# Turning x of eight pairs with transposing transfers instead of TensorE

## The chip, the cores and the metric

The kernel runs on one core of a Trainium2 chip. The metric is device time in microseconds, as the median of several runs; smaller is better. Besides these runs there is one execution taken by the profiler, from which every duration below comes.

## What is computed

Two steps, one behind the other. Attention within chunks of 64 tokens, and then a token mixer without a softmax:

```python
# q, k, v: (8 batches, 8 heads, 576 tokens, 64)
scores = scale * np.matmul(q_c, k_c.transpose(0, 1, 2, 4, 3))   # per chunk of 64
attn = softmax(scores)                                          # 1e-9 is added to the sum
out = np.matmul(attn, v_c)                                      # back to (8, 8, 576, 64)
# x: heads side by side, (8, 576, 512)
wq, wk = x @ w_q, x @ w_k                                       # 512 -> 64
W_tok = scale * np.einsum('bsd,btd->bst', wq, wk)
mixed = np.einsum('bst,btd->bsd', W_tok, x)
y = np.maximum(mixed, 0.0) @ w_out                              # (8, 576, 512) float32
```

## The kernel before

**Pairs.** The work is cut into twenty pairs `u` (a batch and a block of 256 tokens, two "blocks" of 128 each). Two batches give five pairs: two whole pairs of the first, one rest pair that holds the last 64 tokens of both, two whole pairs of the second. So 2, 7, 12 and 17 are the rest pairs, and 8 and 9, 10 and 11, 13 and 14, 15 and 16 are the whole pairs of batches 3, 4, 5 and 6.

**Steps of a pair.** `turns` brings q and k into SBUF with the head dimension on the partitions (turned on TensorE, L379, copied out of PSUM as `qbd` and `kt`). `attention` makes the scores on TensorE (L400), the row maximum and the subtraction on VectorE (L413, L424, L420 for rest pairs), the exponential on ScalarE (L434), turns the exponentials on TensorE (L446), copies them out as `et`, multiplies by v in two steps for a whole pair (L477), and after each step computes denominator, reciprocal and product on VectorE (L490, L494, L504). The products are `xs[u]`, f16, 128 tokens x 2 blocks x 512 features.

**The projection.** `project` needs x with features on the partitions. For each pair its inner function `turn` makes a TensorE step `xT` (L528, eight 128x128 transposes into PSUM) and a copy `xt` out of PSUM by ScalarE or VectorE. The pairs of one batch share one `xt` tile. Step `pj` (L545) multiplies it by `wqk` in four matmuls; `wt`, `wkT` and `wkn` follow.

**Mixing.** `mixing` makes the gram matrix of a batch on TensorE (L599) and copies it as `g16`; `mix_out` makes the mix in two halves (L639) and the relu `rm`; `outs` makes the outputs (L688, four matmuls a group), copies them into one of eleven `osb` buffers, and `send` issues the stores: two for each whole pair (L711) and two for each rest pair (L705), nearly all from SyncE.

**Order.** Nothing is scheduled at run time. Every step gets a number in the order in which it is created, and the string `ORDER` lists all steps: `p` on TensorE, `a` on ScalarE, `v` on VectorE, `s` a send on SyncE, `t` a send on ScalarE's queue, `i` a filler matmul. The number behind `p` is the PSUM bank. Each engine runs its steps strictly in the order of this list and waits for what a step needs. The last lines of the function read it:

```python
    for e in ORDER.split():
        what, eng, *at = re.split(r"([ipavst])", e, maxsplit=1)
        ...
        n.emit(*{"p": (), "a": ("ACT",), "v": ("DVE",)}[eng])
```

**Loads.** The string `LOADS` orders the loads of q, k and v (`Q8`, `K8`, `v8`: of pair 8), which GpSimd issues and which cast from f32 to f16 on the way. A load is issued as soon as its buffer has been read by the pair that held it, in that order and no other.

Of the kernel before, what the change touches and what calls it, by code (L numbers as in the profile page):

```python
# [11 lines left out]
F32 = mybir.dt.float32  # L12
# [58 lines left out]
1v 0a i7.256 i6.256 i5.256 i7.256 i6.256 i5.256 i7.256 i6.256 i5.256 i7.256 i6.256 i5.256 i7.256 i6.256 i5.256  # L71
i7.256 i6.256 i5.512 i7.256 i6.256 7p0 8v 3a 2v 6a 9a i7.512 i6.512 i5.512 i7.512 i6.512 i5.512 i7.256 10p1 11a
i7.512 i6.512 i5.512 i7.256 12p0 26p7 13v 29p6 88p5 14v 28a 27a 30a i4.512 i3.512 i2.512 i4.512 91p7 15a i6.256
31p0 92v 32v 89a i6.512 i3.512 i7.512 53p4 16p7 33v 17a 56a i3.512 i2.512 18p6 90a 54v 22p2 19v 23v 34a 24v 55v
20v 25v i1.512 i0.512 57p4 93p0 58v 35p5 21v 107p2 36a 59v 45p3 109a 94v 110p5 108a 60a i4.512 41p6 95v i2.256
61p4 111a 62a 46a i2.512 63p4 96a 37p0 64v 42v 65v 38v 43v i2.512 153p3 39v 44v 97p2 155a 40v 112p6 66v 47p0
98a 154a 113v 67p2 156p1 68a 48a i5.512 69p2 114v 157a 49p0 158p4 70v 50v 115a 159v 103p2 71p0 99p6 72a 51p0
116p1 52a 4a 172p0 117a 104v 160v 100v 175p1 73p4.5 173v 105v 174a 101v 106v 176a 102v 74v 75a 118p6 122p0 5a
78p4 161a 123v 119v 124v 125v 120v 76p2 77a 121v 126p0 199p1 79v 177p6 200a 128p2 127a 178v 162p3 202a 129a
163a 201a 130p2 179v 131a 180a 203p3 84p1 204v 82p2 205v 85a 168p6 206a 132p3 181p1 169v 83v 164p4 170v 182a  # L80
234p2 165v 133v 166v 171v 134p3.1 236a 167v 235a 183p6 136a 187p4 135a 191p2 188v 184v 189v 207p3 190v 185v
139p0 137p4 140a 192v 186v 138v 237p2 253p6 208a 238a 209p0 255a 193p7 210v 239p4 211v 194a 212v 256p2 254a
240v 213p7 195p6 214a 257v 149p0 241v 215p7 145p2 216a 196a 217p7 150v 242a 258p4 218v 302p6 259v 299p7 303a
318p3 300a 146v 86p6 301a 260v 320a 197p2 304p0 198a 243p7 319a 305v 87a 87s 244a 143p2 345p3 306v 219p6.4 348a
144a 321p7 347v 221a 220a 249p0 245p4 261a 346v 246v 250v 80p6 251v 247v 248v 322a 349p3 81a 81s 323p4 222p6
350v 223a 252v 262p2 351v 224p0 263a 324v 147p3 225a 272p6 325v 380p2 273a 383p7 352a 382v 268p4 264p0 265v
151p6 381a 266v 269v 270v 267v 384a 230p2 326a 271v 385p0 274p7 353p4 231v 307a 386v 327p2 275a 308p5 328a
276p7 354v 309a 387v 148a 148s 314p4 277a 226p2 315v 316v 152a 152s 317v 278p7 310p0 279a 333p4 227a 311v 399p6
334v 312v 335v 313v 280p7.3 402p2 336v 281v 329p0 403a 355p4 330v 228p7 337p2 401a 331v 356v 332v 357v 282a
338a 400a 358v 339p3 283p0 285p4 340v 284v 359p2 286a 341p6 232p3 360v 388a 342v 295p4 404p0 296a 343p6 361p2  # L90
405v 141p4 344a 362a 363p2 448p6 142a 142s 364v 406v 365p2.5 229a 229s 464p4 449a 233v 233s 445p7 367a 366a
407a 389p5 447v 368p2 446v 370p0 390a 369v 289p6 371a 408p5 466v 395p2 409a 391p0 376p7 392v 465a 396v 393v
397v 394v 450p4 398v 377a 290a 467p0 451v 410p2 468a 414p6 374p1 411v 412v 452v 297p0 375a 418p1 453a 413v
469p4 415v 416v 293p2 419a 417v 470v 454p1 491p3 420p6 471v 298a 298s 455a 291p7 421a 294a 493v 460p4 456p0
472a 492v 422p2 457v 458v 494v 459v 495p3 423a 287p6 461v 462v 496v 424p2 473p0 425a 497v 378p1 474a 463v 498a
475p2 288v 288s 479p4 379a 379s 526p0 480v 292a 292s 481v 426p1.6 482v 529p7 476v 427a 428v 527a 477v 429p4
478v 530a 483p6 430v 528a 431p2 499p7 432a 531p0 484v 545p4 532v 548p5 500a 546a 501p6 485p2 549a 502v 533v
439p3 547a 486a 550p4 503v 504v 534a 372p2 551v 441p6 535p0 505p1 373a 373s 442a 552v 487p2 506a 536a 507p1
488a 508v 537p4 541p6 553a 538v 542v 509p2 489p1 437p0 490v 539v 543v 440a 540v 554p1 510a 544v 511p2.3 555a
438a 438s 556p6 560p4 512v 513a 561v 564p1 557v 558v 562v 516p2 565a 435p0 559v 563v 517a 514p6 566p1 515v  # L100
433p2 567a 568p1 443p3 569a 434a 570p1 524p6 444a 444s 571v 436a 436s 572p1.7 522p0 574v 573a 525v 577p2 575p6
523a 523s 578a 520p0 576v 518p1 521v 581p6 583p0 519a 519s 584a 584s 579p1 580v 582a 582s 589p2 587p0 585p6
590a 591p1 586a 592v 588a 588s 592s 586t
"""


# [1 line left out]
def kernel(  # L108
# [10 lines left out]
    nc = tc.nc  # L119
# [3 lines left out]
    C, P, R, G = 64, 128, 2, 32  # L123
    NF = DM // P
# [23 lines left out]
    wqk = const.tile([P, NF, 2, DH], F16, name="wqk")  # L148
# [3 lines left out]
    wo = const.tile([P, NF, DM], F16, name="wo")  # L152
# [22 lines left out]
    def home(tag, shape, dtype=F16):  # L175
        return work.tile(shape, dtype, name=tag, tag=tag, bufs=HOMES[tag])
# [116 lines left out]
    def either(n):  # L293
        return {"ACT": act(n), "DVE": vec(n)}
# [4 lines left out]
    def copy(eng, to, of):  # L299
        (nc.vector.tensor_copy if eng == "DVE" else nc.scalar.copy)(to, of)  # L300

    st, xs = {}, {}
# [210 lines left out]
    def project(us):  # L513

        b, m = pairs[us[0]]
        ni = 1 if m is None else 2
        wide = len(us) * ni * P
        bp, bw = Banks(1), Banks(1)
        made = []

        def turn(n, u):
            bt = Banks(1)

            def pe_t():
                tx = in_banks(bt, ni * NF * C, F16)[:, 0].rearrange("p (f i s) -> p f i s", f=NF, i=ni)
                for i in range(ni):
                    for f in range(NF):
                        nc.tensor.transpose(tx[:, f, i, :], xs[u][:, i, 2 * f : 2 * f + 2, :], ident[:])  # L528
# [188 lines left out]
    for u, (b, m) in enumerate(pairs):  # L717
        made = turns(u)
# [23 lines left out]
_INS = ['q', 'k', 'v', 'moe_w_q', 'moe_w_k', 'moe_w_out']  # L742
_OUTS = [((8, 576, 512), 'float32')]
# [25 lines left out]
```

## Time and profile before

| | |
|---|---|
| median of 3 runs | 137.56 us (137.22 to 137.69) |
| the profiled execution's own time | 137.94 us |
| its span, first to last instruction | 136.1 us |
| mean granted TensorE clock | 0.994 |
| TensorE busy | 121.7 us, 89% |
| VectorE busy | 109.3 us, 80% |
| ScalarE busy | 100.5 us, 74% |
| GpSimd busy (issuing loads) | 74.5 us, 55% |
| transfers | 25.08 MB, mean 184 GB/s |
| SyncE's queue (hardware_dynamic) | 7328 packets, 10.36 MB |
| GpSimd's queue (software_dynamic) | 78752 packets, 14.29 MB |

Busy time is the union of an engine's instructions; matmuls overlap one another, so their mean duration is longer than the step from one to the next. The chain of waits gives the step: each piece of it is the time for which that line held the end back. In the profile, PE is TensorE, PEld its weight load, DVE VectorE, ACT ScalarE, POOL GpSimd, and SPq SyncE's queue. A row of a group ends with the idle time of its engine just before it, and with what ended that idleness.

### The profile page before, as it was taken

How to read it: one execution, taken by the hardware profiler on the slowest of the kernel's cores; microseconds unless marked ns; L12 is line 12 of the kernel's file. 1: busy time of each engine (PE TensorE's matmuls, PEld its weight loads, DVE VectorE, ACT ScalarE, POOL GpSimd, SP SyncE). 2: the span in 40 equal slices, each digit the busy share in tenths (PEclk: the TensorE clock that was granted, in tenths of full speed). 3: DMA queues.
4: the chain of work that ended last, by engine and by line, in shares of the span. 5: the costliest groups of instructions: out<-in, count | busy, mean ns of one | idle time of the engine just before them, and what ended most of it. 6: DMA issues, size and time to landing. Idle time of an engine off the chain costs nothing.

```text
span 136.1 us, 4949 instructions
## 1 busy us (share of the span) xinstructions
PE 121.7 (89%) x2120; PEld 82.6 (61%) x2120; DVE 109.3 (80%) x210; ACT 100.5 (74%) x175; POOL 74.5 (55%) x96
## 2 busy tenths in 40 slices
PE   6998879986899999999999999996999999999910
PEld 4565656865646677676668667663568766544500
DVE  5635999999898899999999979999699998636220
ACT  6358469867998777998995789865878999576600
POOL 7966989978987859995539348935600000000000
PEclk9999999999999999999999999999999999999997
DMA  3999999999999999999999999999999833619883
GB/s 85 284 180 163 172 165 172 165 168 180 174 173 171 181 175 165 175 161 245 256 176 178 281 165 152 177 242 255 202 176 225 282 76 98 154 37 250 269 256 113
DMA packets 86245, 25.08 MB, mean 184 GB/s; under 512 B 78928, under 2 KB 81744, under 8 KB 86224
## 3 DMA queue, kind: packets, MB, share of 16 engines
q0 software_dynamic: 78752, 14.29, 129.5%
q1 hardware_dynamic: 7328, 10.36, 25.7%
q8 instruction: 16, 0.26, 0.7%
q10 hardware_dynamic: 144, 0.13, 0.3%
q14 instruction: 5, 0.04, 0.1%
HBM read 29.62 MB, written 9.44 MB: 287 GB/s over the span
## 4 chain that ended last, share of the span: by engine, by line
PE 60%; DVE 13%; ACT 10%; DMA 6%; issue 5%; POOL 2%; POOLq 0%; DVEq 0%; ACTq 0%
PE ps L688 22%; PE ps L379 7%; DMA qk<-in_q_dram 6%; PE ps L528 5%; PE ps L477 5%; PE ps L400 4%; PE ps L545 4%; PE ps L639 4%; DVE xs L504 4%; PE ps L446 3%; ACT es L434 2%; DVE mx L413 2%; PE ps L599 2%; PE ps L732 2%; ACT et L300 1%
## 5 line engine op out<-in xcount | busy, mean ns | idle before, releaser
L688 PE MATMUL ps<-wo,rm 128*128 128x512 f16 (+1 forms) x148 | 35.8, 374 | 0.1
L230 POOL DMA_DIRECT2D v_all<-in_v_dram x33 | 28.7, 882 | 10.4 <-PE ps L528 4.2
L413 DVE TENSOR_REDUCE mx<-ps 128x16 f32<-128x1024 f32 (+1 forms) x20 | 22.2, 1108 | 3.0 <-PE ps L400 3.0
L504 DVE TENSOR_TENSOR xs<-ps,rec 128x512 f16<-128x512 f32 x36 | 23.9, 684 | 0.4
L434 ACT ACTIVATE es<-sh 128x1024 f16<-128x1024 f32 (+1 forms) x20 | 19.3, 972 | 1.8 <-DVE sh L424 1.7
L688 PEld LDWEIGHTS <-rm 128*128 128x128 f16 x148 | 13.1, 98 | 12.2 <-issue 0.4
L379 PE MATMUL ps<-ident,qk 128*64 128x128 f16 x512 | 19.4, 221 | 1.2 <-DMA qk<-in_q_dram 0.6
L424 DVE TENSOR_TENSOR sh<-ps,mx 128x1024 f32<-128x1024 f32 x16 | 19.6, 1224 | 0.5
L300 ACT COPY osb<-ps 128x512 f32<-128x512 f32 (+1 forms) x28 | 15.3, 574 | 4.6 <-PE ps L688 4.0
L379 PEld LDWEIGHTS <-qk 128*64 128x64 f16 x512 | 15.8, 110 | 4.5 <-DMA qk<-in_q_dram 1.3
L300 ACT COPY qbd<-ps 64x512 f32<-64x512 f32 (+1 forms) x28 | 15.7, 565 | 2.9 <-PE ps L379 1.7
L216 POOL DMA_DIRECT2D qk<-in_q_dram x15 | 13.6, 908 | 4.1 <-PE ps L379 1.6
L216 POOL DMA_DIRECT2D qk<-in_k_dram x15 | 13.5, 902 | 3.6 <-DMA qk<-in_k_dram 2.7
L661 ACT ACTIVATE rm<-ps 128x1024 f16<-128x1024 f32 (+1 forms) x12 | 13.7, 1138 | 2.0 <-PE ps L639 1.8
L300 ACT COPY et<-ps 128x512 f32<-128x512 f32 (+1 forms) x19 | 10.4, 550 | 5.5 <-PE ps L446 5.3
L732 PE MATMUL ps<-ones 128*128 128x512 f16 (+1 forms) x48 | 11.9, 383 | 1.2 <-DVE ones L155 1.2
L400 PEld LDWEIGHTS <-qbd 128*128 128x128 f16 x288 | 10.4, 98 | 3.5 <-DVE qbd L300 0.9
L446 PE MATMUL ps<-ident,es 128*128 128x128 f16 x144 | 11.2, 219 | 1.3 <-issue 1.3
L400 PE MATMUL ps<-kt,qbd 128*128 128x64 f16 x288 | 11.5, 193 | 0.7 <-DVE qbd L300 0.5
L528 PE MATMUL ps<-ident,xs 128*128 128x128 f16 x144 | 11.2, 220 | 0.9 <-DVE xs L504 0.9
L477 PE MATMUL ps<-v_all,et 64*64 64x65 f16 x576 | 10.4, 195 | 1.8 <-DVE xs L504 1.1
L477 PEld LDWEIGHTS <-et 64*64 64x64 f16 x576 | 7.8, 107 | 6.6 <-issue 2.6
(56 smaller groups left out, 177.1 us busy)
## 6 DMA issues: line engine op xcount, KB each, us to landing
out_dram<-osb SPq DMA_DIRECT2D x31, 256.0 KB, 4.5
v_all<-in_v_dram POOLq DMA_DIRECT2D x31, 128.0 KB, 6.7
qk<-in_q_dram POOLq DMA_DIRECT2D x15, 256.0 KB, 7.9
qk<-in_k_dram POOLq DMA_DIRECT2D x15, 256.0 KB, 8.0
out_dram<-osb SPq DMA_DIRECT2D x9, 128.0 KB, 4.1
v_all<-in_v_dram POOLq DMA_DIRECT2D x10, 64.0 KB, 7.8
osb<-in_q_dram SPq DMA_DIRECT2D x1, 512.0 KB, 4.1
osb<-in_k_dram SPq DMA_DIRECT2D x1, 512.0 KB, 5.1
```

Of the source, the lines that this page charges most:

```text
L216: nc.gpsimd.dma_start(qk[u][:, t], rows)
L230: nc.gpsimd.dma_start(v_all[on, slot[u] + i, :, 0:D], v[b, :, of, :].rearrange("h p d -> p h d"))
L300: (nc.vector.tensor_copy if eng == "DVE" else nc.scalar.copy)(to, of)
L379: nc.tensor.transpose(tp[half(o), j, :, r, :], of, ident[:])
L400: nc.tensor.matmul(sp[:, i, j, c ^ turned(u, i), :], lhsT=st["qb", u][:, j, x].rearrange("p o s -> p (o s)"), rhs=st["kt", u][:, j, x * C ...
L413: nc.vector.tensor_reduce(mx[:], scores(), axis=AX.X, op=ALU.max)
L424: nc.vector.tensor_tensor(out=sh[:].rearrange("p x (g r) -> p x r g", r=R), in0=in_banks(bs, 512).rearrange("p i (x r g) -> p (i x) r g", ...
L434: nc.scalar.activation(es[:].rearrange("p x s -> p (x s)"), st["sh", u][:].rearrange("p x s -> p (x s)"), AF.Exp, scale=scale_attn,)
L477: nc.tensor.matmul(to[half(k ^ i), i if ni == 2 else w, x, :], lhsT=et[half(k), i, h // 2, h % 2, :], rhs=v_all[half(k), slot[u] + i, h, 0:W],
L504: nc.vector.tensor_tensor(out=to, in0=xp()[:, :, :, 0:D], in1=by, op=ALU.mult)
L528: nc.tensor.transpose(tx[:, f, i, :], xs[u][:, i, 2 * f : 2 * f + 2, :], ident[:])
L688: nc.tensor.matmul(in_banks(bo, wide)[:, 0], lhsT=st["rm", key][:, f, at_tok + i * P : at_tok + i * P + P], rhs=wo[:, f, s], start=(f == 0 ...
```

## The change

For the pairs 8, 9, 10, 11, 13, 14, 15 and 16 the step `xT` on TensorE and the copy `xt` are replaced by one step `xd`: two transposing transfers issued by SyncE, one for each block of 128 tokens, which read `xs[u]` and write the same `xt` tile, SBUF to SBUF. Each moves 128 x 512 f16 values, 128 KB. The other twelve pairs are turned as before. In `ORDER` such a step has the letter `d`. There are eight steps fewer, so the numbers behind the first carried pair differ from those before. The lists `LOADS` and `ORDER` are new in full; the engines that copy out of PSUM are chosen anew with them, and there are 45 fillers where there were 48.

```diff
+CARRIED = (8, 9, 10, 11, 13, 14, 15, 16)
...
-LOADS = "Q1 K1 Q3 K3 Q2 K2 v0 Q4 K4 v1 v2 Q5 K5 wqk v3 Q6 K6 v4 Q7 K7 wo v5 Q8 v6 K8 Q9 v7 K9 Q10 K10 Q11 Q12 K11 K12 v8 Q13 K13 v9 v10 v11 Q14 K14 v12 Q15 K15 Q16 v13 K16 v14 Q17 K17 v15 Q18 v16 K18 v17 Q19 K19 v18 v19 "
+LOADS = "Q1 K1 Q3 K3 Q2 K2 Q4 K4 v0 v1 Q5 K5 v2 v3 Q6 K6 wqk v4 Q7 K7 v7 Q8 K8 v5 v6 Q9 K9 Q10 K10 wo Q12 Q11 K12 K11 v8 Q13 K13 Q17 v9 v10 v11 Q14 v12 K14 Q15 K15 K17 Q16 K16 v13 v17 v14 v15 Q18 v16 K18 Q19 K19 v18 v19 "
...
+        def room(n, u):
+
+            if ("xt", us[0]) not in st:
+                st["xt", us[0]] = home(f"xt{ni}", [P, NF, wide])
+            return st["xt", us[0]][:, :, n * ni * P : n * ni * P + ni * P]
+
         def turn(n, u):
+            if u in CARRIED:
+
+                def carry():
+                    for i in range(ni):
+                        to = room(n, u)[:, :, i * P : i * P + P]
+                        nc.sync.dma_start(to, xs[u][:, i].rearrange("p h d -> p (h d)"), transpose=True)
+
+                made.append(add("xd", {"SP": 1.0}, carry, st["x_n", u]))
+                return
             bt = Banks(1)
...
-                copy(eng, to, in_banks(bt, ni * NF * C)[:, 0].rearrange("p (f s) -> p f s", f=NF))
+                copy(eng, room(n, u).bitcast(F32), in_banks(bt, ni * NF * C)[:, 0].rearrange("p (f s) -> p f s", f=NF))
...
-        what, eng, *at = re.split(r"([ipavst])", e, maxsplit=1)
+        what, eng, *at = re.split(r"([ipavstd])", e, maxsplit=1)
...
-        n.emit(*{"p": (), "a": ("ACT",), "v": ("DVE",)}[eng])
+        n.emit(*{"p": (), "d": (), "a": ("ACT",), "v": ("DVE",)}[eng])
```

Of the new `ORDER`, the stretches around the four places where the projection takes carried pairs. Pairs 8 and 9 (`268p0` is the last v step of pair 9, `152v` and `152s` the copy and the send of rest pair 2, `274p1` the projection), then 10 and 11 (`337p4`):

```text
321p4 264p2 219p0.7 221a 379p1 80p7 220a 380a 268p0 322v 347v 323v 348a 81a 81s 324a 224p4 269v 270v 265v 271v 266v 267v
349p7 151p6 325p0 222p2 152v 152s 225a 350a 326a 223a 312p4 351p6 352v 313v 353v 314v 315v 354v 147p1 86p0 272d
273d 308p4 331p6 327p2 148v 148s 332v 333v 309v 328v 329v 334v 310v 330v 311v 87a 87s 274p1 230p0 381p6 382v
275a 398p1 395p4 276p5 355p2 439p3 399a 277a 383v 396a 397v 278p5.1 279v 280v 356a 357p2 400p6 440a 384a 231a
441a 226p5 283p0 336d 335d 337p4 385p3 401v 402v 284a 293p6 358a 338a 227v 294v 281p0 141p5 359p4 339p2 282a
```

Pairs 13 and 14 (`285p5` the last outputs of pair 8, `286a` and `286s` their copy and send, `416p5` the projection), then 15 and 16 (`473p6` the last v step of pair 16, `479p3` the projection):

```text
487p6 374p7 373a 449a 285p5 286a 286s 414d 415d 464v 488v 465v 518p4 454p2 450p0 416p5 489v 466a 467p6 455v
451v 456v 452v 453v 417v 490a 491p0 295p1 457v 492v 519a 468a 520a 418p6 469p2 493p4 419a 296a 296s 375a 375s
420p6.0 521p1 421a 422a 473p6 470v 494v 471v 495v 472v 496v 474v 475v 425p2 476v 522a 426a 523p0 524v 289p4
537p5 540p2 423p6 368p3 539a 538a 541a 497p5 478d 477d 525v 424v 542p0 431p2 543v 526a 369a 369s 290a 290s 432a
498a 479p3 480a 527p4 499p5 427p2 500a 501p5 481p3 435p6 544v 545a 528v 502v 482v 436a 529p0 533p4 546p3
```

More of the change, by code (lines that the diff above doesn't have):

```diff
@@ L72 @@
[L72 to L101, printed above, removed]
@@ new lines @@
+95v 34a i6.512 i1.256 57p7 5v 111a i6.512 18p0 22p2 23v 19v 35p4 24v 20v 58v 59v 96a 108a 36a 97p6 21v 41p4
+i7.512 37p0 42v 25v 38v 45p7 112p2 60a 39v 43v 40v 44v 113v 153p4 156p5 i1.256 61p0 155a 154a 62v 63p0 47p4
+114v 64v 98a 46a 99p6 103p2 48v 157a 115a 175p4 172p5 174a 100v 104v 105v 65v 106v 101v 102v 66v 158p6 159v
+160v 116p0 117a 176a 173a 126p1 67p2 49p3 122p4 123v 68a 50a 118p6 51p0 119v 124v 125v 120v 121v 4v 69p3 70a
+199p2 177p4 128p3 71p6 178v 161a 127a 234p1 162p7 201a 179v 202v 200v 236v 72a 52a 129a 163a 130p3 131v 73p0.4
@@ new lines @@
+168p6 180a 132p5 181p3 237p2 182a 133a 74a 238a 169v 75v 235v 170v 171v 203p1 204v 183p4 134p0.3 187p6 135a
+136a 205v 188v 189v 190v 184v 76p0 164p2 165v 185v 166v 137p6 77a 206a 138a 167v 186v 239p0 207p2 78p4 191p3
+256p6 208a 257a 297p2 299a 298a 192a 300p7 240v 241v 79v 253p6 149p0 139p4 209p2 254v 255v 210v 301a 150a 193p7
+302p0 242a 140a 211v 212v 82p6 213p2 303v 316p3 258p4 194a 83a 318a 214v 304v 259v 317v 84p7 341p6 243p2 85a
+215p7 216v 305a 6a 244a 260v 145p0 217p7 342v 218v 146a 195p3 249p4 245p0 196a 250v 246v 251v 343v 247v 248v
@@ new lines @@
+306p7 143p3 197p2 319p0 376p1 261a 252v 307v 344v 144a 262p3 345p6 346v 320a 198a 378a 263a 377a 321p4 264p2
+219p0.7 221a 379p1 80p7 220a 380a 268p0 322v 347v 323v 348a 81a 81s 324a 224p4 269v 270v 265v 271v 266v 267v
+349p7 151p6 325p0 222p2 152v 152s 225a 350a 326a 223a 312p4 351p6 352v 313v 353v 314v 315v 354v 147p1 86p0 272d
+273d 308p4 331p6 327p2 148v 148s 332v 333v 309v 328v 329v 334v 310v 330v 311v 87a 87s 274p1 230p0 381p6 382v
+275a 398p1 395p4 276p5 355p2 439p3 399a 277a 383v 396a 397v 278p5.1 279v 280v 356a 357p2 400p6 440a 384a 231a
@@ new lines @@
+441a 226p5 283p0 336d 335d 337p4 385p3 401v 402v 284a 293p6 358a 338a 227v 294v 281p0 141p5 359p4 339p2 282a
+386a 340v 442p6 458p7 460v 360a 443a 361p4.3 444p0 445v 403a 363a 142a 142s 362a 228p6 459a 229a 229s 232p3
+404p2 364p4 446v 387p0 233v 233s 388v 389v 390v 405v 365a 366p6 461p3 462v 367a 447a 287p4 391p0 406p6 410p2
+288v 411v 412v 392v 393v 394v 291p5 370p4 483p0 413v 407v 408v 484v 485v 409v 371a 292a 463p2 486a 372p4 448p5
+487p6 374p7 373a 449a 285p5 286a 286s 414d 415d 464v 488v 465v 518p4 454p2 450p0 416p5 489v 466a 467p6 455v
@@ new lines @@
+451v 456v 452v 453v 417v 490a 491p0 295p1 457v 492v 519a 468a 520a 418p6 469p2 493p4 419a 296a 296s 375a 375s
+420p6.0 521p1 421a 422a 473p6 470v 494v 471v 495v 472v 496v 474v 475v 425p2 476v 522a 426a 523p0 524v 289p4
+537p5 540p2 423p6 368p3 539a 538a 541a 497p5 478d 477d 525v 424v 542p0 431p2 543v 526a 369a 369s 290a 290s 432a
+498a 479p3 480a 527p4 499p5 427p2 500a 501p5 481p3 435p6 544v 545a 528v 502v 482v 436a 529p0 533p4 546p3
+503p6.7 534v 530v 535v 531v 536v 532v 428a 547a 505a 504v 552p2 548p4 553v 549v 554v 550v 555v 551v 429p7 508p0
@@ L104 @@
+556p6 506p2 558p4 433p5 557v 559a 509a 560p4 437p6 561a 430a 507v 562p4 516p0 434v 434s 430s 563a 564p7.1 438a
+438s 517a 565v 566v 514p0 515v 515s 567p6 569p4 512p1 568a 570v 513a 510p0 511a 511s 581p4 582v 577p1 579p6
+575p0 571p7 583p4 573p5 576v 572v 580a 580s 576s 578v 578s 584a 574v 574s 584t
 """
```

10 lines of the change are left out of this document (4 added, 6 removed).

## The prediction

> **What bounds the kernel now.** I read the page first, then busy time by stretch, the chain of work that ended last, the groups by form, and last SyncE's own queue with its transfers. In the groups by form, "128x512 f16 x36 | 23.9, 684" means 36 instructions, 23.9 us busy together, 684 ns each.
>
> ```profile
> span 136.1 us, 4949 instructions
> PE 121.7 (89%) x2120; PEld 82.6 (61%) x2120; DVE 109.3 (80%) x210; ACT 100.5 (74%) x175; POOL 74.5 (55%) x96
> PE 60%; DVE 13%; ACT 10%; DMA 6%; issue 5%; POOL 2%; POOLq 0%; DVEq 0%; ACTq 0%
> ```
>
> The same by stretch (columns: PE, PEld, DVE, ACT, POOL busy with counts, clock, DMA share, GB/s):
>
> ```profile
> 0.00:40.00 40.00, 34.20 (x626) 24.07 (x627) 32.10 (x60) 28.47 (x49) 34.17 (x47) 1.00 1.84 173
> 40.00:130.00 90.00, 87.49 (x1496) 58.55 (x1494) 76.70 (x152) 72.03 (x127) 40.32 (x49) 1.00 1.50 190
> ```
>
> From 40 to 130 us TensorE is busy 87.49 of 90 us: it runs one step after the other in the order of the list and waits 2.5 us in all. So whatever leaves TensorE's list there is worth its time, and whatever makes TensorE wait there costs its time. All eight carried pairs lie in that stretch. These are the prices of TensorE's steps, as the chain of waits lists them (start, time on the chain, what):
>
> ```profile
> 55.65 0.47 PE ps L400 x16
> 56.12 0.45 PE ps L446 x8
> 56.56 0.86 PE ps L688 x4
> 62.55 0.43 PE ps L639 x2
> 63.86 0.45 PE ps L528 x8
> 70.55 0.25 PE ps L477 x16
> 73.03 0.55 PE ps L599 x10
> 73.58 0.45 PE ps L379 x16
> 77.33 0.22 PE ps L528 x4
> 77.56 0.86 PE ps L545 x4
> 97.28 0.97 PE ps L545 x4
> 104.53 0.22 PE ps L446 x4
> ```
>
> In names: scores 0.47, turning the exponentials 0.45 (0.22 for a rest pair), a group of outputs 0.86, half a mix 0.43, turning x 0.45 (0.22), half of attention times v 0.25, the gram matrix 0.55, turning q or k 0.45, the projection 0.86.
>
> **What is removed.** Eight pairs lose their eight transposes: 8 x 0.45 = 3.6 us off TensorE, on the path. They also lose one eviction each, six of them on ScalarE:
>
> ```profile
> L300 ACT COPY xt<-ps 128x512 f32<-128x512 f32 x13 | 7.6, 585 | 1.6 <-PE ps L528 1.5
> PE ps L545 <- ACT xt L300: 0.3, 1, 0.3
> ```
>
> 6 x 0.585 = 3.5 us of ScalarE, beside TensorE's other work: in the whole run the projection waited for this eviction once, 0.3 us. I count these at nothing. If ScalarE or VectorE waits are smoothed too, the most that can come back is the 2.5 us of idleness above.
>
> **What is added.** Sixteen transfers of 128 KB on SyncE's queue, two a pair, four ahead of each of four projections. The projection is the next step on TensorE that needs them, and everything behind it in the list waits with it. No transposing transfer is in this trace. Its nearest rows are the stores of the same queue: first their issue, then issue to landing while loads still run (57 to 95 us) and while they end (95 to 122 us), then the extremes.
>
> ```profile
> 70.91 1.25 SPq L711 DMA_DIRECT2D out_dram<-osb  x2
> 72.25 1.27 SPq L705 DMA_DIRECT2D out_dram<-osb  x2
> 127.60 0.37 SPq L707 DMA_DIRECT2D out_dram<-osb  x1
> ```
>
> ```profile
> out_dram<-osb SPq DMA_DIRECT2D x12, 256.0 KB, 6.9
> out_dram<-osb SPq DMA_DIRECT2D x4, 128.0 KB, 6.2
> ```
>
> ```profile
> out_dram<-osb SPq DMA_DIRECT2D x11, 256.0 KB, 4.0
> out_dram<-osb SPq DMA_DIRECT2D x2, 128.0 KB, 2.3
> ```
>
> ```profile
> DMA to landing us min/median/max: 2.2/4.4/9.0
> ```
>
> So one issue takes 0.63 us (0.37 at the least), three ahead of the last one 1.9 us, and the landing L of a 128 KB store is 6.2 us beside the loads and 2.3 us without them. A transposing transfer stays inside SBUF, which may make it quicker than a store (I go down to 1 us), or it moves in smaller pieces, which may make it slower (up to the 9.0 us of the slowest store). I take the row of the same size and hour. What must pass before the four can be issued is read from the order, with these prices:
>
> ```profile
> L504 DVE TENSOR_TENSOR xs<-ps,rec 128x512 f16<-128x512 f32 x36 | 23.9, 684 | 0.4
> L424 DVE TENSOR_TENSOR sh<-ps,mx 128x1024 f32<-128x1024 f32 x16 | 19.6, 1224 | 0.5
> L413 DVE TENSOR_REDUCE mx<-ps 128x16 f32<-128x1024 f32 x16 | 19.5, 1217 | 3.0 <-PE ps L400 3.0
> L300 ACT COPY osb<-ps 128x512 f32<-128x512 f32 x26 | 14.7, 589 | 4.3 <-PE ps L688 3.7 <-PE ps L561 0.6
> L494 DVE RECIPROCAL rec<-den 128x8 f32<-128x8 f32 x36 | 6.3, 192 | 0.7 <-DVE den L490 0.2
> L300 DVE COPY osb<-ps 128x512 f32<-128x512 f32 x9 | 6.2, 684 | 3.8 <-ACT osb L300 2.5 <-PE ps L688 1.2
> L490 DVE TENSOR_SCALAR den<-ps 128x8 f32<-128x8 f32 x36 | 5.2, 159 | 2.7 <-PE ps L477 2.0 <-ACT g L323 0.3
> L420 DVE TENSOR_TENSOR sh<-ps,mx 128x512 f32<-128x512 f32 x4 | 2.7, 686 | 0.1
> ```
>
> **Pairs 8 and 9 (272d, 273d, projection 274p1).** Time counts from the end of 268p0, the last v step of pair 9. TensorE then has mix 0.43, turning 0.22, output 0.86, turning 0.45, mix 0.43, two v steps 0.5, two outputs 1.72, three v steps 0.75: 5.4 us, then the projection. VectorE first ends a max and two subtractions (1.22 + 0.69 + 1.22 = 3.1), the first of which could start when the scores step 321p4 ended; TensorE's steps from there to the end of 268p0 are 0.25 + 0.55 + 0.45 + 0.86 + 0.25 = 2.4, so it is 0.8 us late. Then two denominators, two reciprocals and two products (2.1) and the output copy 152v (0.68), since SyncE's list has 152s, the send of that copy, ahead of 272d: 3.5. The send is two issues, 1.27: 4.8. Three issues 1.9: 6.7. Then L. TensorE waits 6.7 + L - 5.4 = L + 1.3. The loads are at their thickest here, L = 6.2: **7.5 us**.
>
> **Pairs 10 and 11 (336d, 335d, projection 337p4).** By the same clock VectorE's products for them end at 3.5 + 2.1 + 0.7 + 3.1 = 9.4, and SyncE, after 273d (7.3) and the two sends 148s and 87s, is free at 9.8; its last of four issues starts at 11.7 and lands at 11.7 + L. TensorE, after waiting, starts 274p1 at 6.7 + L and has then at least 0.86 + 0.86 + 0.47 + 0.9 + 0.22 + 0.45 + 0.55 + 0.47 + 0.86 + 0.43 = 6.1 us before 337p4: 12.8 + L. Whatever L is, these land 1.1 us in time: **0**, hidden by the wait before. If that cover went, L - 5.2 would show, which is 1.0 us.
>
> **Pairs 13 and 14 (414d, 415d, projection 416p5).** SyncE has 286s ahead, whose last copy 286a can begin only when output step 285p5 ends. From there: copy 0.59, two issues 1.27, three issues 1.9, L: 3.8 + L. TensorE has turning 0.45 and two v steps 0.5, 0.95. It waits L + 2.8. In the run before, this projection began at 97.28 us, where the loads are ending; I take L = 5, between 6.2 and 4.0: **7.8 us**.
>
> **Pairs 15 and 16 (478d, 477d, projection 479p3).** From the end of v step 473p6 TensorE has 0.43 + 0.47 + 0.86 + 0.9 + 0.43 + 0.86 + 0.22 + 0.47 + 0.86 = 5.5 us. VectorE needs between one denominator, reciprocal and product (1.0) and three of each (3.1); I take 1.9, then 1.9 of issue, then L, and all loads are down: L = 3, a little over 2.3. The wait is L - 1.7: **1.3 us**, between 0 and 4.
>
> **The rest.** Behind the transfers on SyncE's queue stand sends (148s, 87s; 296s, 375s; 369s, 290s); nobody on TensorE waits for a send but through the eleven output buffers, and the last sends come long after. They cost nothing. The 2 MB share the engines with the loads; TensorE's waits above give the loads more time than they lose. The loads' order and the first steps are rearranged, with 45 fillers for 48. TensorE is idle 5.8 us in the first 40; the new head I count at 0, between -2 and +3. Counted over both lists, VectorE gets some copies that ScalarE had: about 5 us more on an engine busy 76.7 of 90 us, covered by the waits.
>
> **Sum.** The profiled execution took 137.94 us around its span of 136.1, 0.4 above the median 137.56. 137.94 - 3.6 + 7.5 + 0 + 7.8 + 1.3 = 150.9, so 150.5 for the runs that are timed. The likeliest case with its own range is 147 to 153.
>
> **Two rules weighed.** The trace prices eight turns at 0.45 us on TensorE and has none by transfer. The Trainium skill, "VectorE: DVE Perf Modes", section "The three transpose paths", gives 1309 ns for one 128x128 block by DMA against 390 ns on TensorE, and the rules under it advise TensorE where PSUM will do as the destination. A transfer here holds four blocks; estimated from that page, L lies between 1.3 (overlapped) and 5.2 (one by one), and the sum would be 141.0 or 152.3.
>
> The second is TensorE's clock, which falls in the trace:
>
> ```profile
> 129.00:130.00 1.00, 0.78 (x4) 0.17 (x2) 0.18 (x1) 0.60 (x2) 0.00 (x0) 1.00 0.83 270
> 134.00:134.50 0.50, 0.00 (x0) 0.00 (x0) 0.00 (x0) 0.00 (x0) 0.00 (x0) 1.00 0.67 172
> 134.50:135.00 0.50, 0.00 (x0) 0.00 (x0) 0.00 (x0) 0.00 (x0) 0.00 (x0) 0.59 0.01 4
> ```
>
> The last matmul ends at 129.8, and between 134.5 and 135 the granted clock drops to half: some 4.8 us of idleness do it. The waits of 7.5 and 7.8 us are longer. The Trainium skill, "TensorE: Matmul & The Clock Gate", section "What's actually happening", has the clock halved after an idle window of about 3.4 us and back after as long a busy one; estimated by that, two such waits lose 1.7 us each, 154.3 in the sum. The drop agrees in size; the return no row here shows.
>
> **Rivals.** *Quick transfers hidden (faster).* The three waits total 2L + 4.1 for small L; with all 2.5 us of idleness recovered the sum is even at L = 1.0, and at L = 0.5 with issues of 0.37 us (three of them 1.1 instead of 1.9, so 0.8 less at each of two places) 137.94 - 3.6 - 2.5 + 1.0 + 2.5 = 135.3. For: nothing goes to HBM. Against: no store landed under 2.2 us. Chance 0.05. *Short landing:* L = 2.3 everywhere: waits 3.6 + 5.1 + 0.6, 143.6; for it the rows after 95 us, against it those before. Chance 0.23, as 141 to 147. *Half clock:* each long wait is followed by matmuls at half speed; if that lasts as long as the fall took, 2.4 us each are lost, 155.7. Chance 0.15. *Slower than a store:* L = 9 twice, then 4: 10.3 + 11.8 + 2.3 of waits, 158.7. Chance 0.14. *The waits cancel against 3.6 us:* 0.02. The forecast keeps 0.41. Both high rivals reach from 153 to 160. 142 to 160 leaves out some 0.15.
>
> A difference under 0.3% can't be told from none here. Slower by more: 0.41 + 0.23 + 0.15 + 0.14 = 0.93; the same 0.02; faster 0.05.
>
> **What would show it.** TensorE should lose 64 of the 144 turns of L528, and the waits list should name L545 waiting for transfers into xt, two waits of 6 to 9 us, one of 1 to 2, one of none; SyncE should issue each first transfer right after the send ahead of it. Wrong would be: transfers that land under 2 us, a projection that starts without waiting, SyncE's issues over 1 us each, or VectorE as the releaser of TensorE's waits.

## The result and the profile after

The changed kernel takes 168.14 us (166.09 to 168.36, 4 runs) against 137.39: the ratio is 1.2207, with a 95% interval of 1.2142 to 1.2273. The forecast was slower, 150.5, within 142 to 160: the direction held, and the time lies beyond the range. The profiled execution is the quickest of the four, 166.09 us, with a mean granted clock of 0.94; the other three had 0.91. Where executions of one kernel fall into a quicker and a slower group, its ratio below is that of the quicker group.

First the page after: span, busy time, granted clock in forty slices, and the chain that ended last.

```profile
span 164.3 us, 4844 instructions
PE 122.6 (75%) x2053; PEld 80.1 (49%) x2053; DVE 113.9 (69%) x221; ACT 92.6 (56%) x156; POOL 74.5 (45%) x96
PEclk9999999999999999998559999999758999999996
PE 34%; DMA 19%; DVE 15%; SPq 12%; POOL 7%; issue 4%; ACT 4%; POOLq 0%; DVEq 0%
```

TensorE's share of the chain fell from 60% to 34%; transfers and SyncE's queue have 31%. The clock goes to half in two places. The waits of TensorE name the cause, and its timeline the places (start, length, what, and in brackets the idle time before it and its releaser):

```profile
PE ps L558 <- DMA xt<-xs: 23.1, 4, 10.6
PE ps L380 <- DMA qk<-in_k_dram: 2.7, 3, 2.0
```

```profile
83.83 1.87 PE L558 MATMUL ps<-xt,wqk 128*128 128x512 f16 x4 [10.55 <-DMA xt<-xs]
94.56 1.04 PE L558 MATMUL ps<-xt,wqk 128*128 128x512 f16 x4 [1.75 <-DMA xt<-xs]
121.05 1.86 PE L558 MATMUL ps<-xt,wqk 128*128 128x512 f16 x4 [7.81 <-DMA xt<-xs]
136.48 1.02 PE L558 MATMUL ps<-xt,wqk 128*128 128x512 f16 x4 [3.02 <-DMA xt<-xs]
```

All four projections with carried pairs waited: 10.55, 1.75, 7.81 and 3.02 us. The forecast had 7.5, 0, 7.8 and 1.3. SyncE's timeline shows what stood in front:

```profile
70.20 1.13 SPq L718 DMA_DIRECT2D out_dram<-osb  x2
71.37 6.10 SPq L534 DMA_TRANSPOSE xt<-xs  x4
77.59 2.67 SPq L724 DMA_DIRECT2D out_dram<-osb  x4
80.38 7.00 SPq L534 DMA_TRANSPOSE xt<-xs  x4
101.41 12.55 SPq L724 DMA_DIRECT2D out_dram<-osb  x8
114.07 5.74 SPq L534 DMA_TRANSPOSE xt<-xs  x4
130.04 5.20 SPq L534 DMA_TRANSPOSE xt<-xs  x4
```

Two stores take 1.13 us to issue, four transposing transfers 5.2 to 7.0. From issue to landing, the first eight (71 to 88 us) and the next four (114 to 120 us):

```profile
L534 SPq DMA_TRANSPOSE xt<-xs x8: 1226/1364/2446, 71.4 to 84.9; - x8
DMA to landing us min/median/max: 7.7/8.3/9.6
```

```profile
L534 SPq DMA_TRANSPOSE xt<-xs x4: 1211/1264/1811, 114.1 to 118.5; - x4
DMA to landing us min/median/max: 2.3/2.4/3.6
```

So a transposing transfer takes at least 1.21 us to issue, twice a store, and lands in 2.4 us or in 8.3, by when it goes. Landing counts from the start of the issue: the last transfer of the third group starts at 118.5, and TensorE's wait for it ends at 121.05.

### The profile page after: what moved, and what is told of

It is laid out like the page before. It is cut to its first block, busy times and chain, and to the rows that moved or that the text cites. A ratio compares the mean times of both kernels' runs of the same rounds, so it can differ in the third digit from the quotient of the medians.

```text
span 164.3 us, 4844 instructions
## 1 busy us (share of the span) xinstructions
PE 122.6 (75%) x2053; PEld 80.1 (49%) x2053; DVE 113.9 (69%) x221; ACT 92.6 (56%) x156; POOL 74.5 (45%) x96
## 4 chain that ended last, share of the span: by engine, by line
PE 34%; DMA 19%; DVE 15%; SPq 12%; POOL 7%; issue 4%; ACT 4%; POOLq 0%; DVEq 0%
PE ps L701 15%; DMA qk<-in_k_dram 10%; SPq L534 10%; DMA xt<-xs 9%; PE ps L652 4%; DVE mx L414 3%; POOL qk L217 3%; PE ps L558 3%; DVE xs L505 3%; PE ps L380 3%; PE ps L447 3%; POOL v_all L231 3%; DVE sh L425 2%; SPq L724 2%; PE ps L478 2%
## 5 line engine op out<-in xcount | busy, mean ns | idle before, releaser
L414 DVE TENSOR_REDUCE mx<-ps 128x16 f32<-128x1024 f32 (+1 forms) x20 | 22.0, 1110 | 15.2 <-PE ps L401 15.2
L558 PE MATMUL ps<-xt,wqk 128*128 128x512 f16 (+1 forms) x48 | 11.5, 366 | 23.1 <-DMA xt<-xs 23.1
L380 PE MATMUL ps<-ident,qk 128*64 128x128 f16 x512 | 18.7, 221 | 4.4 <-DMA qk<-in_k_dram 2.7
L301 ACT COPY qbd<-ps 64x512 f32<-64x512 f32 (+1 forms) x24 | 13.5, 561 | 11.5 <-PE ps L380 10.9
L380 PEld LDWEIGHTS <-qk 128*64 128x64 f16 x512 | 15.4, 110 | 8.6 <-DMA qk<-in_k_dram 3.7
L301 ACT COPY osb<-ps 128x512 f32<-128x512 f32 (+1 forms) x26 | 14.6, 578 | 7.6 <-PE ps L701 7.5
L674 ACT ACTIVATE rm<-ps 128x1024 f16<-128x1024 f32 (+1 forms) x14 | 16.8, 1207 | 3.1 <-PE ps L652 3.0
L558 PEld LDWEIGHTS <-wqk 128*128 128x128 f16 x48 | 3.9, 102 | 27.3 <-issue 23.3
L301 ACT COPY et<-ps 128x512 f32<-128x512 f32 (+1 forms) x15 | 8.2, 553 | 11.7 <-PE ps L447 11.6
L301 ACT CAST wt<-ps 128x512 f16<-128x512 f32 (+1 forms) x9 | 4.3, 481 | 17.7 <-PE ps L558 17.6
L478 PE MATMUL ps<-v_all,et 64*64 64x65 f16 x576 | 11.3, 196 | 2.3 <-ACT et L301 0.7
L478 PEld LDWEIGHTS <-et 64*64 64x64 f16 x576 | 8.6, 106 | 8.7 <-issue 4.9
```

The costliest lines, as they stand in the source:

```text
L380: nc.tensor.transpose(tp[half(o), j, :, r, :], of, ident[:])
L414: nc.vector.tensor_reduce(mx[:], scores(), axis=AX.X, op=ALU.max)
L478: nc.tensor.matmul(to[half(k ^ i), i if ni == 2 else w, x, :], lhsT=et[half(k), i, h // 2, h % 2, :], rhs=v_all[half(k), slot[u] + i, h, 0:W],
L558: nc.tensor.matmul(in_banks(bp, wide)[:, 0], lhsT=wqk[:, f].rearrange("p i j -> p (i j)"), rhs=st["xt", us[0]][:, f, :], start=(f == 0), s ...
L674: nc.scalar.activation(to, of, AF.Relu, scale=scale_moe)
```

## The experiments

In every kernel that reads ones, the projections of the eight pairs get a tile of ones for the turned x, so it leaves out what would be computed from x there. Diffs are cut; `...` stands for what is left out, and for long stretches of a list.

**1. The lists alone (e_list).** What do the new lists cost when no transfer is issued?

```diff
-                    for i in range(ni):
+                    for i in range(0):
...
-                    rhs=st["xt", us[0]][:, f, :],
+                    rhs=ones[:] if us[0] in CARRIED else st["xt", us[0]][:, f, :],
```

> The changed kernel's two lists with neither transposes nor transfers for the eight pairs: their projections read a tile of ones instead of the turned x, so the values computed there are left out. Theory (the four waits for the transfers are the loss): without them TensorE has 3.6 us of turns and 1.2 us of fillers less and some 3 us more idleness in the first 60 us than before, so 137.4 - 4.8 + 3.2 = 135.8, between 134 and 139. Rival (the new lists are slow in themselves, for instance by the order of the loads): above 145. Rival (the lists are good and only the first part lost): 133 or less.

Measured: 140.2 us, ratio 1.0229 (1.0172 to 1.0285). Neither end: the 27.9 us between this and the changed kernel are the transfers', but the lists without turns are 2.7 us slower than the kernel before, which does all turns. TensorE's busy time by stretch, here and before (first column after the length):

```profile
0.00:60.00 60.00, 50.31 (x987) 35.86 (x988) 52.84 (x99) 39.76 (x68) 49.62 (x66) 1.00 1.86 170
```

```profile
0.00:60.00 60.00, 53.73 (x1030) 38.29 (x1031) 50.88 (x96) 44.94 (x80) 50.82 (x67) 1.00 1.91 173
```

It idles 9.7 us in the first 60, against 6.3, long before the first carried pair.

**2. The old lists without the eight turns (b_noturn).** The most that the removal can bring in the old order.

```diff
-... 272p6 ... 273a ...     # xT and xt of the eight pairs leave ORDER
+    rhs=ones[:] if us[0] in CARRIED else st["xt", us[0]][:, f, :],
```

> The kernel before with its own two lists, less the eight transposes and the eviction of each of the eight pairs; their projections read a tile of ones, so the values computed there are left out. It is the most that taking these turns off TensorE could bring in this order. Theory (TensorE's work is the bound): 3.6 us less than 137.4, so 133.5 to 134.5. Rival (another engine or the loads hold the end as soon as TensorE has less to do): 136 or more. Against the 140.2 of the changed lists without turns it gives the price of the new lists: 6 us by the theory.

Measured: 136.75 us, ratio 0.994 (0.9905 to 0.9975). The rival holds. TensorE's busy time from 40 us on, and the chain that ended last:

```profile
40.00:130.00 90.00, 84.63 (x1432) 55.05 (x1429) 76.12 (x149) 69.25 (x120) 40.23 (x49) 1.00 1.50 191
```

```profile
DVE 39%; PE 23%; DMA 13%; ACT 11%; issue 7%; POOL 1%; SPq 1%; DVEq 0%; POOLq 0%; ACTq 0%
```

TensorE does 2.9 us less work there than before (87.49), and idles more for it: VectorE now has 39% of the chain, where it had 13%. Removing 3.6 us from the busiest engine was worth 0.8 us (0.3 to 1.3 by the interval); by the chain it is VectorE, close behind, that holds the end now. With 140.2 it puts the price of the new lists at 3.4 us, or 4.0 by the two ratios.

**3. Transfers nobody waits for (e_unwaited).** The transfers are issued as in the change; the projections read ones.

> The changed kernel with all sixteen transposing transfers issued where they were, into their tiles, but with projections of the eight pairs that read a tile of ones: nobody on TensorE waits for a transfer, and the values computed there are left out. Theory (the waiting is the loss): 140 to 142.5, the 140.2 of the lists without transfers plus up to 2 us for loads and sends that are delayed. Rival (sharing the transfer engines and SyncE's queue with loads and stores costs in itself): above 146.

Measured: 145.4 us, by one execution (a second took 148.5). Between the two theories, and nearer to the rival: sharing costs some 5 us over the lists alone. Its largest sum of waits of TensorE:

```profile
PE ps L476 <- DMA v_all<-in_v_dram: 4.5, 5, 1.3
```

The loads of v come late: in e_list these waits were 0.7 us. In the changed kernel they are 0.4, as TensorE is waiting for the transfers meanwhile.

**4. Earlier in SyncE's queue (e_early).** Each `d` stands right behind the pair's last product, ahead of the sends that stood between.

```diff
-... 152v 152s ... 147p1 86p0 272d
-273d 308p4 ...
+... 252v 272d 307v ... 267v 273d 349p7 151p6 325p0 222p2 152v 152s ...
...
-... 286s 414d 415d ...
+... 394v 414d ... 409v 415d ... 286s ...
```

> The changed kernel with each pair's two transfers moved up in SyncE's queue to the place right behind the pair's last product, ahead of the output sends that stood before them. Theory (issue and landing behind the sends): pair 8 is issued long ahead, the last of pairs 8 and 9 starts near 71 and lands near 79, so the first wait falls from 10.6 to about 6; the second stays at 0 to 1.8; the third falls from 7.8 to under 1 (products done at 109.9, projection reached at 113.2, two issues and a landing of 2.4); the fourth from 3.0 to under 1. 23.2 us of waits become about 7, and the half clock after the third goes: 166 - 16 - 1.6 = 148, between 144 and 152. Rival (the transfers are slow by themselves, wherever they stand in the queue): the waits shrink by less than 5 us in all, above 161.

Measured: 159.8 us (159.1 and 160.4), ratio 1.1657 (1.1541 to 1.1773). Better by 8 us, not by 20, and between the two theories. The waits (the last row shows three of its four matmuls):

```profile
79.01 1.87 PE L556 MATMUL ps<-xt,wqk 128*128 128x512 f16 x4 [5.55 <-DMA xt<-xs]
89.99 1.02 PE L556 MATMUL ps<-xt,wqk 128*128 128x512 f16 x4 [1.32 <-DMA xt<-xs]
115.83 1.44 PE L556 MATMUL ps<-xt,wqk 128*128 128x512 f16 x3 [7.19 <-DMA xt<-xs]
```

The first fell to 5.55 as expected, the fourth is gone, and the third stayed at 7.19 though its transfers went 11 us earlier. Their landing (103 to 107.5 us) says why:

```profile
L532 SPq DMA_TRANSPOSE xt<-xs x4: 1232/1266/1815, 103.0 to 107.5; - x4
DMA to landing us min/median/max: 7.8/8.5/8.8
```

In the changed kernel the same transfers landed in 2.4 us. Moved ahead, they met the last loads; experiment 5 tests that.

**5. No loads for the pairs from 10 on, order untouched (e_fewloads), and with the earlier transfers (e_early_few).** This takes the backlog away and leaves the transfers; these pairs compute on the data of earlier pairs.

```diff
+    ALIAS = {10: 3, 11: 4, 12: 7, 13: 5, 14: 6, 15: 8, 16: 9, 17: 2, 18: 1, 19: 3}
...
+        if u in ALIAS:
...
+            continue
...
+        if u in ALIAS:
+            qk[u] = qk[ALIAS[u]]
```

> The changed kernel with its order untouched and no loads of q, k and v for the pairs from 10 on, which compute on the data of earlier pairs (their results are left out). Theory (the backlog of loads sets the landing): all landings 2.3 to 3.7 us, the first wait falls from 10.6 to about 5, the second to 0, the third and fourth stay at 7.8 and 3.0 as their transfers landed quickly already: 16 us of waits, 158 to 162. Rival (landing depends on the transfers' own queue): the first landing stays over 6 us and the time over 165.

> The kernel with the transfers moved up, and no loads of q, k and v for the pairs from 10 on: those pairs compute on the data of earlier pairs, so their results are left out. The loads then end near 60 us, before the first transposing transfer. Theory (what makes a transfer take 8 to 10 us instead of 2.4 is the backlog of loads): all sixteen land in 2.3 to 3.7 us; the waits then are at most 1 us at pairs 8 and 9 and none elsewhere, and the time comes back to that of the lists without turns, 140.2, give or take 2. Rival (the thickness of SyncE's own queue, transfers behind transfers and stores, makes the 8 us): landings stay over 6 us in the first two groups and the time over 148.

Measured: e_fewloads 161.3 us, ratio 1.1737 (1.1678 to 1.1796); e_early_few 145.0 us (144.5 and 145.5), ratio 1.0561 (1.0474 to 1.0648). The landings of all sixteen and TensorE's waits for them, first in e_fewloads, then in e_early_few:

```profile
DMA to landing us min/median/max: 2.3/2.4/4.1
```

```profile
PE ps L564 <- DMA xt<-xs: 14.6, 3, 7.8
```

```profile
DMA to landing us min/median/max: 2.3/2.4/3.9
```

```profile
PE ps L564 <- DMA xt<-xs: 4.0, 3, 1.7
```

Landing 2.4 us at the median wherever the transfers stand: the loads' backlog makes the 8 us, and neither turning nor the queue's own stores do. Of 23.1 us of waits, leaving the loads out takes 8.5, and moving the transfers ahead as well 10.6 more. The theory of e_fewloads held, though the time fell by less than the waits: TensorE's busy time is 127.0 us there, 7.5 above e_list, through more time at half clock (experiment 8). e_early_few came out between its two theories. The 4.0 us of waits that stay there (1 at most was expected) are the issues and the landing behind the last product; ahead of pair 16's transfers two sends, 296s and 375s, also still stand in SyncE's list.

**6. Plain copies in place of turning (e_plain).**

```diff
-nc.sync.dma_start(to, xs[u][:, i].rearrange("p h d -> p (h d)"), transpose=True)
+nc.sync.dma_start(to, xs[u][:, i].rearrange("p (f o) d -> p f (o d)", o=2))
```

> The changed kernel with the same sixteen transfers as plain copies of the same size and shape, without turning: x is not turned for the eight pairs. Theory (half of the loss beyond the forecast is the price of issuing a transposing transfer, 1.27 us against 0.63): each last issue starts 1.9 us sooner and the landings stay near those of a store, so the waits become about 8, 0, 6 and 1, 15 to 17 us instead of 23.2, and the time 158 to 161. Rival (any transfer of 128 KB behind the loads costs that much): within 2 us of the changed kernel's. Rival (turning makes the transfer itself slow): landings under 3 us beside the loads, and a time below 150.

Measured: 160.0 us, by one execution (a second took 164.0). The theory held.

```profile
L532 SPq DMA_DIRECT2D xt<-xs x16: 594/656/1943, 71.0 to 128.2; - x16
DMA to landing us min/median/max: 2.2/5.3/9.7
```

The landings are those of the transposing ones (2.3, 5.6 and 9.6 over all sixteen). Turning costs 0.6 us per issue and nothing that shows in the landing. Four groups of shorter issues took TensorE's waits for `xt` from 23.1 us to 15.4, and the profiled execution is 6 us shorter.

**7. Halves and wholes (e_halves, e_one).** Does the issue cost go by size? Each transfer cut into two of 64 KB, or one of 256 KB for each pair.

```diff
+for g in range(2):
+    nc.sync.dma_start(to[:, 2 * g : 2 * g + 2], xs[u][:, i, 4 * g : 4 * g + 4]..., transpose=True)
```

> The changed kernel with each transposing transfer cut into two of 64 KB. Theory (an issue has a fixed part like a store's, 0.63 us, and a part that grows with the tiles it turns): 0.95 us each, a group of eight 7.6 us against 5.1, the waits 2.5 us longer each, 173 to 177. Rival (all of the issue's price is by size): 0.64 us each, and 166 to 169. Rival (all of it is fixed): 1.27 us each, 10 us a group and over 180.

> The changed kernel with one transposing transfer of 256 KB a pair in place of two of 128 KB; the blocks of 128 tokens stand outermost in the tile for that, and the projection reads it with a stride. Theory (issuing costs 1.25 us whatever the size, as the halves showed): two issues a group, so the last one starts 2.5 us sooner; the waits become about 8, 0, 5.5 and 0.5 instead of 10.6, 1.8, 7.8 and 3.0, and the time 157 to 160. Rival (over some size the issue grows with it): issues of 2 to 2.5 us and a time within 2 us of the changed kernel's.

Measured: e_halves 185.1 us (one run), e_one 164.3 us (163.7 and 165.0), ratio 1.1916 (1.1800 to 1.2031). The issues of each:

```profile
L533 SPq DMA_TRANSPOSE xt<-xs x32: 1189/1243/2299, 71.9 to 152.1; - x32
```

```profile
L534 SPq DMA_TRANSPOSE xt<-xs x8: 1261/2026/4401, 71.2 to 130.3; - x8
DMA to landing us min/median/max: 3.3/7.0/11.6
```

64 KB cost 1.24 us as 128 KB do, so the price is fixed there: of the three forecasts for e_halves the last one held. With 256 KB it is 1.26 at the least and beside the loads up to 4.4, and the landing is 1 to 2 us longer (2.3, 5.6 and 9.6 for 128 KB): the first wait stayed at 10.95 us, the others fell by 1.1 to 1.8. So e_one came out between its two theories.

**8. TensorE kept busy (e_warm).** Fillers of 512 columns in front of three of the projections.

```diff
-274p1
+i1.512 (44 times) 274p1          # and 32 before 416p5, 10 before 479p3
```

> The changed kernel with filler matmuls of 512 columns put on TensorE right before three of the waiting projections (44, 32 and 10), so that it works instead of idling; they end before the transfers land. The granted clock should then stay at 1.00 throughout. Theory (the wait is the loss, the half clock a small part): the 3.1 us at half clock after the first wait are hidden by the second wait, which a transfer sets, and only those after the third wait come back: 1.6 us, so 164.5 to 167 against 168. Rival (the half clock is a main part, 5.7 us by the rise of TensorE's busy time): 161 to 163.

Measured: 165.7 us (164.5 and 166.8), ratio 1.2086 (1.192 to 1.2252). The stretch around the first long wait in this kernel, and single microseconds of the changed one:

```profile
73.00:87.00 14.00, 10.30 (x92) 4.74 (x78) 2.93 (x10) 0.48 (x1) 5.29 (x7) 1.00 1.75 176
```

```profile
76.00:77.00 1.00, 0.00 (x0) 0.00 (x0) 0.00 (x0) 0.00 (x0) 0.70 (x1) 0.71 1.37 225
...
86.00:87.00 1.00, 1.00 (x7) 0.38 (x6) 0.00 (x0) 0.32 (x1) 0.87 (x1) 0.67 1.30 273
...
117.00:118.00 1.00, 0.00 (x0) 0.00 (x0) 0.00 (x0) 0.00 (x0) 0.00 (x0) 0.69 0.60 135
...
124.00:125.00 1.00, 1.00 (x8) 0.46 (x7) 0.65 (x2) 0.96 (x2) 0.00 (x0) 0.90 0.00 0
```

The granted clock is the third figure from the end of a row. In the changed kernel it falls from 1.00 to 0.50 within the microseconds from 76 and from 117, and returns within those from 86 and from 124. A mean of 0.71 puts the fall 0.42 us into its microsecond, at 76.4; likewise 117.4 for the second, and 86.7 and 124.2 for the returns. With the fillers the clock stayed full, and 2.5 us came back, as the theory had it (with intervals that overlap those of the changed kernel, so the size is rough): the half clock is a small part of the loss here.

**9. Two pairs only, in the old lists (e_two, e_two_first).** Only 15 and 16 are carried; in the second kernel three sends go behind pair 16's transfers.

```diff
+CARRIED = (15, 16)
...
-463v 483d 496a 475p2 288v 288s 479p4 379a 379s 524p0 480v 292a 292s ... 478v 484d      # e_two
+463v 483d 496a 475p2 288v 479p4 379a 524p0 480v 292a ... 478v 484d 288s 379s 292s      # e_two_first
```

> The kernel before with its own two lists, in which only pairs 15 and 16 are turned by transposing transfers, each issued right behind its pair's last product; everything else as before. In the trace of before these products end at 100.9 and 103.9, the last load lands at 105.7, and the projection starts at 110.1. Theory (a transfer costs only where its landing is waited for): last issue at 105.2, landing 2.4 to 4 us later near 109, no wait, and TensorE is free of two turns, 0.9 us: 136.5 against 137.4, a ratio of 0.991 to 0.997. Rival (landing beside the last loads takes 8 us): a wait of 3 us and 139 to 140.

> The kernel before with only pairs 15 and 16 carried, as in the run of two pairs, but three sends of two stores each, which stood ahead of pair 16's transfers, are put behind them. There the transfers of pair 16 started at 109.3 because of these stores, with the products done near 104.5. Theory (place in SyncE's queue): they start at 104.5, the last lands at 110 or sooner, the projection at 110.9 does not wait, the clock stays full: 136 to 137.2, a little under the kernel before. Rival (the transfers slow loads, stores or engines otherwise): over 138 although no wait for them shows.

Measured: e_two 142.6 to 144.5 us, ratio 1.0429 (1.036 to 1.0498). The wait and SyncE's queue, in an execution of 145.5:

```profile
PE ps L557 <- DMA xt<-xs: 4.2, 1, 4.2
```

```profile
101.75 2.60 SPq L533 DMA_TRANSPOSE xt<-xs  x2
104.45 4.76 SPq L723 DMA_DIRECT2D out_dram<-osb  x6
109.32 4.16 SPq L533 DMA_TRANSPOSE xt<-xs  x2
```

Neither forecast named it: six stores stood between the two pairs' transfers. e_two_first: 137.6 us, ratio 1.0008 (0.9974 to 1.0041), between its theory and its rival, and SyncE issues

```profile
100.12 6.31 SPq L533 DMA_TRANSPOSE xt<-xs  x4
106.48 5.68 SPq L723 DMA_DIRECT2D out_dram<-osb  x7
```

No wait for `xt` remains, and no time is gained: a hidden carry is worth nothing that can be told here, as b_noturn makes plausible (all eight pairs are worth 0.6%). No kernel tried here beats the one before with the whole computation in it.

**10. What made the new lists cost 3.4 us (e_list_loads, b_noturn_dve, e_list_act).** The old order of loads in e_list; ten copies moved to VectorE in b_noturn; ten copies moved to ScalarE in e_list.

```diff
-LOADS = "Q1 K1 Q3 K3 Q2 K2 Q4 K4 v0 v1 Q5 K5 ..."      # e_list_loads: as before the change
+LOADS = "Q1 K1 Q3 K3 Q2 K2 v0 Q4 K4 v1 v2 Q5 K5 ..."
...
 # b_noturn_dve: four et, four qbd, two kt copies: a -> v; e_list_act: as many v -> a
```

> The changed order with neither turns nor transfers for the eight pairs (their projections read ones, values left out), and with the order of loads of the kernel before. Theory (the new order of the loads, in which v comes ahead of q and k of pairs 4 to 6, makes TensorE wait for q and k near 28 us and is most of what the lists lost): idleness of the first 60 us back from 9.5 to 7.5 us or less, and 137 to 138.5 against 140.2. Rival (the order of the steps is what lost it): 139.5 or more.

> The kernel before less the turns of the eight pairs (their projections read ones, those values left out), with ten copies out of PSUM between 40 and 120 us moved from ScalarE to VectorE: about 6.9 us more work on VectorE, 5.8 less on ScalarE, everything else in the same order. Theory (with less on TensorE, VectorE is the bound, and its extra work is what the new lists cost): 139.5 to 142 against 136.75. Rival (the order of the steps is what they cost): 136 to 138.

> The changed kernel's lists without turns or transfers for the eight pairs (ones in their place, those values left out), with ten copies moved from VectorE to ScalarE, spread over the whole list: about 6.9 us less on VectorE, so that it has less than in the kernel before. Theory (VectorE's extra work is the price of the new lists): 137 to 138.2 against 140.2. Rival (the order of the steps, and the loads in the first 60 us): 139.5 or more.

Measured: e_list_loads 142.0 us, ratio 1.0355 (1.0288 to 1.0421); b_noturn_dve 142.3 us, 1.0312 (1.0232 to 1.0392); e_list_act 143.4 us, 1.04 (1.033 to 1.0471). The engines in the last two:

```profile
PE 119.6 (85%) x2056; PEld 78.9 (56%) x2056; DVE 113.4 (80%) x218; ACT 93.4 (66%) x159; POOL 74.4 (53%) x96
```

```profile
PE 121.7 (86%) x2053; PEld 80.2 (57%) x2053; DVE 109.4 (77%) x211; ACT 95.6 (68%) x166; POOL 74.8 (53%) x96
```

The order of the loads alone is not it: with the old one the new lists are slower still. VectorE's load alone is not it either: b_noturn_dve comes out close to what that theory says, but e_list_act has VectorE back at 109.4 us and is slower than e_list. Each change of one part of a list cost 2 to 5 us by the ratios. Part of that is the clock: it fell in e_list_act too, as its row from 40 to 60 us shows, and TensorE was busy 121.7 us there against 119.5 in e_list (120.5 in e_list_loads).

```profile
40.00:60.00 20.00, 17.14 (x332) 11.79 (x328) 17.16 (x31) 14.95 (x26) 15.21 (x19) 0.91 1.92 177
```

The place of the 3.4 us is on record. In the first 60 us TensorE idles 9.7 us in e_list and 6.1 in b_noturn; after that e_list idles no more than b_noturn (2.1 us from 60 to 131, and 3.1 from 60 to 128). And TensorE waits there for loads, 3.9 us in all, first e_list, then its one such wait in the kernel before:

```profile
PE ps L378 <- DMA qk<-in_k_dram: 2.5, 3, 1.3
PE ps L378 <- DMA qk<-in_q_dram: 0.7, 2, 0.6
PE ps L476 <- DMA v_all<-in_v_dram: 0.7, 1, 0.7
PE ps L379 <- DMA qk<-in_q_dram: 0.6, 1, 0.6
```

With the old order of loads such waits are 3.5 us (e_list_loads). So the new order of steps meets neither order of loads; which step of it is to blame stays open.

## Why the prediction was right and wrong

The step that carried it held: the projection is the next step on TensorE, it waits for issue and landing, and the time grows by the waits. Of the signs, 64 of the turns are gone, L558 waits for transfers into `xt`, and the long waits are at the first and third place. But all four projections waited, where one was to have no wait, and the first waited 10.55 us, where 6 to 9 were named. And one sign of being wrong came: SyncE's issues took over 1 us each.

Against the quickest run, 166.09, the sum made for the profiled execution, 150.9, is 15.2 us short. The terms that failed:

- **The four waits**, 16.6 forecast, 23.1 measured. The issue was taken from a store, 0.63 us, and was 1.2 to 2.4, so the last transfer of a group starts 4.0 to 4.5 us behind the first in place of 1.9. The landing beside loads was taken as 6.2 and was 8.2 in the first group; its first transfer, though, started 1.9 us ahead of TensorE's readiness, where the forecast had 0.6. The third wait came out as forecast, 7.81 for 7.8, by luck: two errors cancel, 2.5 us more of issue and a landing of 2.4 in place of 5. The fourth, 3.02 for 1.3, is the issue again.
- **"Whatever L is, these land 1.1 us in time"** for pairs 10 and 11: wrong, 1.75 us of the 23.1. It used the same L for both groups (9.6 was the second's, 8.2 the first's) and the short issue.
- **The gain.** 3.6 us off TensorE was counted in full, from an engine that waits 2.5 us in 90. It brought 0.8 (experiment 2). The same stretch showed VectorE busy 76.7 of 90; the term should have been bounded by what is late next.
- **The new head and engines**, counted at 0 between -2 and +3: 3.4 us (experiments 1, 2 and 10), as TensorE waits for loads in the first 60 us.
- **The half clock**, kept out of the sum as a rival, at 2.4 us for each long wait. It came, at both, and cost less: TensorE's busy time is 122.6 against 119.5 in e_list, so 3.1 us.

Waits 6.5, gain 2.8, head 3.4 and clock 3.1 make 15.8, against the 15.2 us that were missing. TensorE's clock returned to full 2.8 and 3.2 us after work began again, at 83.83 and 121.05, by the rows of experiment 8. The Trainium skill, "TensorE: Matmul & The Clock Gate", section "What's actually happening", says some 3.4 us. The trace agrees in size only: in e_fewloads, windows of one microsecond put the returns 3.5, 4.1 and 5.5 us after work began. The prediction read "some 4.8 us of idleness do it" off one fall. That is no threshold: the falls here came 3.1 and 4.1 us after TensorE stopped, and the first in e_fewloads 1.9 us after.

Of the rule weighed against the change: the Trainium skill, "VectorE: DVE Perf Modes", section "Rules for kernel authors", advises TensorE for a 128x128 block where PSUM will do. The runs agree in direction. A transfer of four such blocks lands in 2.4 us alone, between the 1.3 and the 5.2 that the prediction estimated.

That all of the transfers would be hidden, or that they land as without loads everywhere, fell with the landings of 8 us. That they are slower than any store (9.0 us) came true only in the second group, 9.6 at the most.

## What to carry to other kernels

Ahead of moving work from an engine to a queue, count three things behind the last producer: what stands before it in that queue, the fixed price of each issue, and the landing at that hour. Here they came to as much as 4.8 us (six stores in e_two), 4.5 us (three issues ahead of the last) and 9.6 us, and a pair was worth 0.1 us by experiment 2. And check what the freed engine would wait for next: this kernel, with 60% of its chain on TensorE and VectorE busy 85% of the time, gave back 0.8 us of the 3.6 removed.

## What the hardware showed beyond the forecast

Issuing a transposing transfer took 1.24 us at 64 KB (median), 1.26 at 128 KB (median of the four from 114 us on) and 1.26 at 256 KB (the least of eight), and a plain one of 128 KB 0.66 (median). Landing went from 2.4 to 8.3 us beside the loads, and for plain copies over much the same range. Sixteen transfers that nobody waited for cost some 5 us (one execution), with 3.8 us more of waits for the loads of v.

TensorE's clock fell in the waits of 10.55 and 7.81 us and not in that of 3.02, but in e_fewloads right behind one of 2.21, and in e_list_act at 18.1 us, after 3 us in which TensorE was busy 1.3. Its spells at half clock lasted 10.2 and 6.8 us in the changed kernel, 6.8, 10.2 and 3.4 us in e_fewloads (74.9 to 81.8, 109.1 to 119.3, 129.6 to 133.0), and 3.4 us twice in e_list_act (18.1 to 21.6, 45.5 to 48.9): one, two or three times 3.4 us. So the length of a wait alone does not tell here whether the clock falls, nor what that costs: 3.1 us in the changed kernel, 7.5 in e_fewloads.
